# Two more pairs of steps with seven block products for the last matrix product, and block sums made from tiles that are already loaded

## The chip, the cores and the metric

The kernel runs on one core of a Trainium2 chip. The metric is the device time of one execution in microseconds (us). Three runs of the kernel before gave 736.80, 737.75 and 737.57 us, a median of 737.57 us.

The engines are named as in the profile. PE is TensorE (matrix products, results in PSUM), DVE is VectorE, ACT is ScalarE, POOL is GpSimd, and SP issues the DMAs. Each engine takes its instructions in a fixed order. One that waits holds up everything behind it on that engine.

## The reference, cut to what matters

```python
attn_out = _attn_ref(x, state)                 # attention both ways, (4, 8, 512+32, 64)
x = attn_out.transpose(0, 2, 1, 3).reshape(B * S, H * D)       # 2176 rows of 512
h = x @ w_in;  g = softplus(h);  x = g @ w_out                 # 512 -> 2048 -> 512
g = x @ w_gate                                                 # 512 -> 1536
silu = g * (1.0 / (1.0 + np.exp(-g)))
val = x @ w_val                                                # 512 -> 1536
return silu * val @ w_out2                                     # 1536 -> 512
```

The 2176 rows are 4 batches of 512 tokens and 128 state rows. The change lies in the last three products, which this text calls the gated stage.

## The kernel before

Every float32 operand is split into a high part and a low part in fp32r, and each product of tiles is three matmuls (high x high, low x high, high x low). The split costs two instructions: a copy on ACT for the high part (`h`) and a subtraction on DVE or POOL for the low part (`l`).

**The gated stage** begins at about 342 us and has 24 steps, numbered n = 0 to 23. Steps 0 to 11 do batches 0 and 1 (p = 0), steps 12 to 23 batches 2 and 3 (p = 1). One step does 128 of the 1536 columns of gate and of value for a pair of batches. It does so by a Strassen-Winograd scheme: seven block products P1 to P7, whose operands from the weights (`gw`) and from the activations (`T`: B11, B21, B22 and the sums T1 to T4) are prepared earlier. Each block product is six matmuls of 128x512, so a step has 42. They accumulate in three PSUM banks `px`, `pz`, `py`, in the order P1, P5, P2, P6, P7, P4, P3. DVE and ACT take the partial results out between them (tiles `cA`, `cB`, `cC`), and Silu and the product of gate and value follow in the next step.

**The last product** of two steps 2k, 2k+1 is done two steps later, in pieces put between the block products. It has two forms. The plain form, `out_mm`, has 24 matmuls in each of the two steps. The form with seven block products, `out_part`, has 18 in the even step (P1, P2, P5, six each) and 24 in the odd step (P6, P3, P7, P4). Its results for the two batches are kept in two pairs of banks: P1, P6, P7 and P4 follow each other in one pair, P2, P5 and P3 in the other, and after each part DVE adds the bank to `oacc`. A part that goes on in a bank can therefore not begin until DVE has read the part before it. This form also needs sums of the activations (`total`, on DVE, lines 994 to 1000 and 985) and sums of four blocks of w_out2 (`w2s`).

Before the change the seven-product form is used for steps 12 to 21, five pairs. The sums `w2s` are made by `OutSums` in steps 10, 12, 13, 14 and 16: two tiles `w2r` are loaded from DRAM, DVE adds high and low parts (`whole`, tiles `w2t`), POOL makes the sums (`w2u`), ACT and POOL split them, and the result is written to DRAM and loaded again by `load_w2s`.

**The sums T1 to T4 of the second pair of batches** are made from the result of the MLP before (`yacc`). `y_sums` does them in steps 9 and 10 (T3 and T2 on DVE, T1 and T4 on POOL); `y_high` and `y_low` split all seven operands in step 11.

**The 128 state rows** run beside steps 0 to 13: `state_1` is their gate and value (12 matmuls of 128x256 a step; Silu and the product are done once for two steps), `state_2` a transposition, `state_3` their last product.

The order on PE is that of the code. DVE, ACT, POOL and SP run in the order in which `run2(n, ...)`, `run_later(n, ...)` and `parts(n, ...)` put instructions between the block products: `conv0` stands after P2, `conv1` before P7, `state` and `conv2` after P7, `conv3` after P3. SBUF and PSUM addresses of the tiles are assigned when the program is built.

Of the kernel before, what the change touches and what calls it, by code (L numbers as in the profile page):

```python
# [37 lines left out]
def attention_moe_moe2_kernel(  # L38
# [38 lines left out]
    SLOTS = {"aT": 8, "mt": 8,  "wo": 6, "yacc": 8, "s": 2, "xT": 8, "T": 14, "made": 3, "w2": 4, "w2s": 4, "gw": 8}  # L77
# [36 lines left out]
    RAWS = {"raw": 2, "raw0": 6}  # L114
# [163 lines left out]
    def load_w2s(q):  # L278
        for k in range(2):
            w2s[q, k] = slot([P, 2, 512], F32R, "w2s", f"w2s{q}_{k}")  # L280
            nc.sync.dma_start(out=w2s[q, k].bitcast(F32), in_=w2s_d[q][:, k])
# [198 lines left out]
    y = {}  # L480
# [28 lines left out]
    def y_sums(p, i, k, eng):  # L509
        b11, b12, b21, b22 = (y_of(2 * p + j, 2 * h + i) for h in range(2) for j in range(2))  # L510
        if k == "T1":
            o = ysum[p, i, k] = b12
        else:
            o = ysum[p, i, k] = work.tile([P, 512], F32, tag="ysum", bufs=6, name=f"{k}_{p}_{i}")
        if k == "T3":
            eng.tensor_tensor(out=o, in0=b22, in1=b12, op=ALU.subtract)
        elif k == "T1":
            eng.tensor_tensor(out=o, in0=b12, in1=b11, op=ALU.subtract)
        elif k == "T2":
            eng.tensor_tensor(out=o, in0=ysum[p, i, "T3"], in1=b11, op=ALU.add)  # L520
        else:
            eng.tensor_tensor(out=o, in0=b21, in1=ysum[p, i, "T2"], op=ALU.subtract)
# [136 lines left out]
    def out_part(n, part):  # L659
# [8 lines left out]
        for i in range(2):  # L668
# [4 lines left out]
            w = w2s[q, k // 2] if kind == "s" else w2[n + int(kind[1])]  # L673
# [7 lines left out]
    def state_1(f):  # L681
        if f % 2 == 0:
            gs["t"] = bank("y", f"pt1{f}").rearrange("p (f s c) -> p f s c", f=2, s=2)
        ps = gs["t"][:, f % 2].rearrange("p s c -> p (s c)")
# [6 lines left out]
        if f % 2:  # L691
            pg, pv = (gs["t"][:, :, s, :] for s in range(2))
            t = work.tile([P, 2, 2 * P], F32, tag="sa", bufs=1, name=f"sa{f}")
            a, g = (t[:, k].rearrange("p (f c) -> p f c", f=2) for k in range(2))
            nc.scalar.activation(a, pg, AF.Silu)
            nc.vector.tensor_tensor(out=g, in0=pv, in1=a, op=ALU.mult)
            gs[f // 2] = t[:, 1]
# [12 lines left out]
    def state_3(q):  # L710
        ps = bank("y", f"pt3{q}")
# [18 lines left out]
    with tc.manual_schedule(engines={ENG.PE}):  # L730
# [244 lines left out]
        def value_times_gate(n, c):  # L975
# [5 lines left out]
            if n < NF or n >= NS2 - 2:  # L981
# [25 lines left out]
        with tc.manual_schedule(engines={ENG.DVE, ENG.SP, ENG.Activation, ENG.Pool}):  # L1007
            run2(-1, "load0")
            run2(-1, "load1")
            for n in range(NS2):  # L1010
# [10 lines left out]
                z = quad_bank(f"pz{n}")  # L1021
                quad_mm(z, n, "P5", True)
                run2(n, "P5")
                y = quad_bank(f"py{n}")
# [16 lines left out]
                else:  # L1041
# [8 lines left out]
                    parts(n, 0) if n >= NF + 2 else outs(n, 0)  # L1050
# [73 lines left out]
```

## Time and profile before

| | |
|---|---|
| median of three runs | 737.57 us |
| the profiled execution | 737.21 us, span 735.4 us |
| granted TensorE clock | 0.995, one core |
| PE busy | 710.3 us (97%) |
| DVE busy | 488.1 us (66%) |
| POOL busy | 441.7 us (60%) |
| ACT busy | 329.0 us (45%) |

The span runs from the first to the last instruction. The execution's own time is 1.8 us longer. A matmul's time in a row includes its way through the array, so a row of three that lists 0.84 us can be followed by the next row 0.68 us later: intervals between starts tell what each one costs. The same holds for DVE, where an instruction with 0.68 us is followed 0.60 us later by the next.

### The profile page before, as it was taken

How to read it: one execution, taken by the hardware profiler on the slowest of the kernel's cores; microseconds unless marked ns; L12 is line 12 of the kernel's file. 1: busy time of each engine (PE TensorE's matmuls, PEld its weight loads, DVE VectorE, ACT ScalarE, POOL GpSimd, SP SyncE). 2: the span in 40 equal slices, each digit the busy share in tenths (PEclk: the TensorE clock that was granted, in tenths of full speed). 3: DMA queues.
4: the chain of work that ended last, by engine and by line, in shares of the span. 5: the costliest groups of instructions: out<-in, count | busy, mean ns of one | idle time of the engine just before them, and what ended most of it. 6: DMA issues, size and time to landing. Idle time of an engine off the chain costs nothing.

```text
span 735.4 us, 10173 instructions
## 1 busy us (share of the span) xinstructions
PE 710.3 (97%) x3610; PEld 561.7 (76%) x3610; DVE 488.1 (66%) x665; ACT 329.0 (45%) x611; POOL 441.7 (60%) x397
## 2 busy tenths in 40 slices
PE   4699999999999999999999999999999999999997
PEld 1367767786777777788887888888888888888886
DVE  5984559888676878466575656665575665675564
ACT  3767445644544545434454434442443434333231
POOL 2467637887556775754396756766767567254352
PEclk9999999999999999999999999999999999999999
DMA  9930215655453535380379987979669997838503
GB/s 342 407 125 0 87 58 172 191 206 176 141 174 138 189 131 180 128 322 1 101 275 356 377 328 269 352 258 328 199 254 379 340 349 280 313 128 326 178 1 115
DMA packets 55395, 159.53 MB, mean 217 GB/s; under 512 B 6192, under 2 KB 18480, under 8 KB 55344
## 3 DMA queue, kind: packets, MB, share of 16 engines
q1 hardware_dynamic: 55344, 158.88, 60.9%
q8 instruction: 28, 0.46, 0.3%
q14 instruction: 23, 0.19, 0.1%
HBM read 117.70 MB, written 41.16 MB: 216 GB/s over the span
## 4 chain that ended last, share of the span: by engine, by line
PE 82%; POOL 3%; issue 2%; ACT 2%; DMA 2%; DVE 1%; SPq 0%; DVEq 0%; ACTq 0%; POOLq 0%
PE py L90 25%; PE px L90 16%; PE ph L90 10%; PE po L90 9%; PE pz L90 8%; PE poP L90 6%; PE pt L90 3%; PE ps L552 2%; PE pm L421 2%; PE ps L90 1%; DMA gv_d<-gv 1%; POOL l L93 1%; DMA raw_gv<-in_moe_w_gate_dram 1%; POOL gv L93 1%; POOL sums_gv L194 1%
## 5 line engine op out<-in xcount | busy, mean ns | idle before, releaser
L90 PE MATMUL py<-h,wo 128*128 128x512 f32 x512 | 158.8, 391 | 2.6 <-DVE yacc L500 1.3
L93 POOL TENSOR_TENSOR l<-C,h 128x512 fp32r<-128x512 f32 x64 | 94.1, 1476 | 78.7 <-PE py L90 51.6
L90 PEld LDWEIGHTS py<-h,wo 128*128 128x128 f32 x512 | 95.9, 188 | 23.9 <-POOL wo L93 2.0
L90 PE MATMUL ph<-aT,m 128*128 128x512 f32 x384 | 101.3, 399 | 1.0 <-DVE m L93 1.0
L90 PE MATMUL py<-l,wo 128*128 128x512 f32 x256 | 99.9, 390 | 0.0
L90 PEld LDWEIGHTS ph<-aT,m 128*128 128x128 f32 x384 | 70.8, 188 | 24.9 <-issue 6.9
L90 PE MATMUL po<-h,w 128*128 128x512 f32 x224 | 69.6, 392 | 0.0
L451 ACT ACTIVATE h<-ph 128x512 fp32r<-128x512 f32 x64 | 38.2, 597 | 68.3 <-PE ph L90 45.9
L90 PE MATMUL px<-T_0s,gw 128*128 128x512 f32 x216 | 60.8, 390 | 0.8 <-ACT cB L1047 0.8
L90 PE MATMUL px<-T_1s,gw 128*128 128x512 f32 x216 | 60.7, 389 | 0.0
L90 PEld LDWEIGHTS py<-l,wo 128*128 128x128 f32 x256 | 48.1, 188 | 10.5 <-POOL l L93 0.3
L90 PEld LDWEIGHTS po<-h,w 128*128 128x128 f32 x224 | 41.6, 188 | 8.4
L635 DVE TENSOR_TENSOR oacc<-po,oacc 128x512 f32<-128x512 f32 x48 | 32.4, 687 | 22.9 <-PE po L90 22.8
L635 DVE TENSOR_TENSOR oacc<-poP,oacc 128x512 f32<-128x512 f32 x62 | 40.7, 686 | 10.3 <-PE poP L90 10.3
L90 PEld LDWEIGHTS px<-T_0s,gw 128*128 128x128 f32 x216 | 40.3, 188 | 9.4 <-ACT cB L1047 1.2
L90 PEld LDWEIGHTS px<-T_1s,gw 128*128 128x128 f32 x216 | 40.6, 188 | 8.5
L93 POOL TENSOR_TENSOR l<-cA,h 128x512 fp32r<-128x512 f32 x14 | 21.4, 1528 | 38.2 <-ACT h L621 38.2
L90 PE MATMUL po<-l,w 128*128 128x512 f32 x112 | 43.6, 390 | 0.0
L93 POOL TENSOR_TENSOR split_gv<-sums_gv,split_gv 128x512 fp32r<-128x512 f32 x24 | 33.0, 1376 | 16.4 <-ACT split_gv L198 16.4
L500 DVE TENSOR_TENSOR yacc<-py,yacc 128x512 f32<-128x512 f32 x48 | 31.3, 685 | 16.7 <-PE py L90 16.7
L93 POOL TENSOR_TENSOR gv<-t_gv,gv 128x512 fp32r<-128x512 f32 x24 | 33.4, 1393 | 14.2 <-issue 11.7
L137 DVE TENSOR_SCALAR t_gv<-t_gv 128x512 int32<-128x512 int32 x24 | 22.1, 920 | 28.2 <-ACT t_gv L133 28.1
(192 smaller groups left out, 1538.5 us busy)
## 6 DMA issues: line engine op xcount, KB each, us to landing
gw<-gv_d SPq DMA_DIRECT2D x96, 512.0 KB, 6.9
gv_d<-gv SPq DMA_DIRECT2D x24, 512.0 KB, 3.9
gv_d<-split_gv SPq DMA_DIRECT2D x24, 512.0 KB, 3.2
w<-w_d SPq DMA_DIRECT2D x24, 512.0 KB, 8.4
raw_win<-in_moe_w_in_dram SPq DMA_DIRECT2D x16, 512.0 KB, 6.9
raw_wo<-in_moe_w_out_dram SPq DMA_DIRECT2D x16, 512.0 KB, 4.1
raw_gv<-in_moe_w_gate_dram SPq DMA_DIRECT2D x48, 128.0 KB, 3.8
raw_gv<-in_moe_w_val_dram SPq DMA_DIRECT2D x48, 128.0 KB, 3.6
```

What stands on the lines that cost most here:

```text
L90: nc.tensor.matmul(o, a[s], b[t], start=first and i == 0, stop=last and i == 2, **k)
L93: eng.tensor_tensor(out=o, in0=whole, in1=high.bitcast(F32), op=ALU.subtract)
L137: nc.vector.tensor_scalar(out=ti, in0=ti, scalar1=3, scalar2=0x7FFFFFF8, op0=ALU.logical_shift_left, op1=ALU.bitwise_and,)
L194: nc.gpsimd.tensor_tensor(out=o, in0=x, in1=y, op=op)
L421: nc.tensor.matmul(ps[k * NS:(k + 1) * NS, :], st[q, k, b, :], win[c, k].t[q, :], start=True, stop=True)
L451: nc.scalar.activation(self.h, self.ps, AF.Softplus)
L500: nc.vector.tensor_tensor(out=v, in0=yps[dt], in1=v, op=ALU.add)
L552: nc.tensor.matmul(ps, sw[:, kt, :], win[c, kt].t, start=kt == 0, stop=kt == KT - 1)
L635: nc.vector.tensor_tensor(out=v, in0=ps, in1=v, op=ALU.add)
```

## The change

The constant `FROM = 8` and `seven(n)` make `out_part` the form for steps 8 to 21, seven pairs instead of five. The pairs 8, 9 and 10, 11 belong to the first pair of batches; their parts run in steps 10 to 13.

`OutSums` no longer loads or stores anything. It reads the tiles `w2[n]`, `w2[n+1]` that are loaded for the last product anyway, and leaves its results in SBUF tiles `w2s`. It runs in the odd step n+1 of each pair: 9, 11, 13, 15, 17, 19, 21. Seven such jobs stand where five were, and the DMAs of `w2r`, `w2o` and `w2s` are gone.

T2 and T4 of the second pair of batches overwrite `yacc`. The sums and splits of that pair are spread over steps 9 to 12 by a table; T4 moves from POOL to DVE, and the tags that share SBUF and PSUM space are changed (`T` 16 slots, `raw2`, `quad_bank`). `state_1` works step by step in a bank of its own, with one Silu and one product of 128x128 in each.

```diff
-        def __init__(self, q):
-            self.q = q
-            self.raw = []
-            for f in range(2):
-                t = slot([P, 2, 512], F32R, "made", f"w2r{q}_{f}")
-                nc.sync.dma_start(out=t.bitcast(F32), in_=w2_d[2 * q + f])
-                self.raw.append(t)
+        def __init__(self, n):
+            self.n = n
 
         def whole(self):
             self.t = []
-            for f, r in enumerate(self.raw):
-                t = rawp.tile([P, 512], F32, tag="tmade", bufs=3, name=f"w2t{self.q}_{f}")
+            for f in range(2):
+                r = w2[self.n + f]
+                t = rawp.tile([P, 512], F32, tag="tmade", bufs=3, name=f"w2t{self.n}_{f}")
                 nc.vector.tensor_tensor(out=t, in0=r[:, 0].bitcast(F32), in1=r[:, 1].bitcast(F32), op=ALU.add)
                 self.t.append(t)
...
         def low(self):
-            w2s_d[self.q] = dram.tile([P, 2, 2, 512], F32, tag=f"w2s{self.q}", name=f"w2s{self.q}_d")
-            for k, o in enumerate(self.o):
+            for k in range(2):
+                o = w2s[self.n, k]
                 low(nc.gpsimd, o[:, 1, :], self.s[k], o[:, 0, :])
-                nc.sync.dma_start(out=w2s_d[self.q][:, k], in_=o.bitcast(F32))
...
@@ y_sums
+        elif p and k in ("T2", "T4"):
+            o = ysum[p, i, k] = b11 if k == "T2" else b21
...
@@ quad_bank
-    def quad_bank(name):
-        banks[0] += 1
-        return bank("h" if banks[0] % 4 else "m", name)
+    def quad_bank(name, state):
+        banks[0] += not state
+        return bank("h" if state or banks[0] % 4 else "m", name)
...
@@ state_1
+        if f % 2 == 0:
+            gs[f // 2] = work.tile([P, 2, 2 * P], F32, tag="sa", bufs=1, name=f"sa{f}")[:, 1]
+        g = gs[f // 2][:, f % 2 * P:(f % 2 + 1) * P]
+        nc.scalar.activation(g, ps[:, :P], AF.Silu)
+        nc.vector.tensor_tensor(out=g, in0=ps[:, P:], in1=g, op=ALU.mult)
...
-                for k, (t, eng) in enumerate((("T3", nc.vector), ("T1", nc.gpsimd), ("T2", nc.vector), ("T4", nc.gpsimd))):
-                    at2(n0 - 3 + i, f"conv{k}", y_sums, p, i, t, eng)
-            for part, (_, t) in PARTS.items():
+                for k, (t, eng) in enumerate((("T3", nc.vector), ("T1", nc.gpsimd))):
+                    at2(n0 - 3 + i, f"conv{2 * k + 1 - i}", y_sums, p, i, t, eng)
+            for t, early, high, then in (
+                ("B11", 1, "P5", "P2"), ("T1", 0, "P5", "P2"), ("B21", 0, "P2", "P6"), ("T2", 0, "P6", "P7"),
...
                 for i in range(2):
-                    at2(n0 - 1, part, y_high, p, i, t)
-                    at2(n0 - 1, part, y_low, p, i, t, nc.gpsimd if t in ("B21", "T3", "B22") else nc.vector)
+                    at2(n0 - 1 - early, high, y_high, p, i, t)
+                for i in range(2):
+                    at2(n0 - 1 - early, then, y_low, p, i, t, nc.gpsimd if t in ("B21", "T3", "B22") else nc.vector)
+            for i in range(2):
+                at2(n0 - 2, "P4", y_sums, p, i, "T2", nc.vector)
+                at2(n0 - 1, "P7", y_sums, p, i, "T4", nc.vector)
...
+        FROM = 8
+        def seven(n):
+            return FROM <= n < NS2 - 2
...
-        for q, n in enumerate((10, 12, 13, 14, 16)):
-            job = {}
-            at2(n - 1, "load1", lambda q=q, job=job: job.update(s=OutSums(q)))
-            for kind, name in (("conv0", "whole"), ("conv1", "sums"), ("conv2", "high"), ("conv2", "low")):
-                at2(n, kind, lambda name=name, job=job: getattr(job["s"], name)())
+        for n in range(0, NS2, 2):
+            if seven(n):
+                job = OutSums(n)
+                for kind, name in (("conv0", "whole"), ("conv1", "sums"), ("conv2", "high"), ("conv2", "low")):
+                    at2(n + 1, kind, getattr(job, name))
...
-            if n < NF or n >= NS2 - 2:
+            if not seven(n):
                 after(n + 1, 1, lambda: split_act((n, 1), c["C"]))
...
-                    parts(n, 0) if n >= NF + 2 else outs(n, 0)
+                    parts(n, 0) if seven(n - 2) else outs(n, 0)
```

Two places show how it moves instructions. The first is the end of step 11 on PE, where the last product of steps 8 and 9 stands. Before, it reads so (`po8_1_2` is the bank for batch 1, third quarter; `px11` takes P4 of the gate product, `pz11` P3, `px12` opens step 12):

```order
L90 MATMUL po8_1_2_5218<-h8_1_4868,w28_4633 128x512 x2
L90 MATMUL po8_1_2_5218<-l8_1_4869,w28_4633 128x512
L90 MATMUL po8_1_2_5218<-h9_1_5018,w29_4635 128x512 x2
L90 MATMUL po8_1_2_5218<-l9_1_5019,w29_4635 128x512
L90 MATMUL po8_1_3_5226<-h8_1_4868,w28_4633 128x512 x2
L90 MATMUL po8_1_3_5226<-l8_1_4869,w28_4633 128x512
L90 MATMUL po8_1_3_5226<-h9_1_5018,w29_4635 128x512 x2
L90 MATMUL po8_1_3_5226<-l9_1_5019,w29_4635 128x512
L90 MATMUL px11_5104<-T4_0_0s_3309,gw11_0_0_4934 128x512 x3
L90 MATMUL px11_5104<-T4_0_1s_3348,gw11_1_0_4936 128x512 x3
L90 MATMUL pz11_5120<-B22_0_0s_3156,gw11_0_1_4938 128x512 x3
L90 MATMUL pz11_5120<-B22_0_1s_3221,gw11_1_1_4940 128x512 x3
```

After, the same place has the parts P7 and P4 (`poP1_8` is the pair of banks that P1 opened; `h8_T3` and `h8_T4` are the split sums of activations):

```order
L90 MATMUL poP1_8_0_5014<-h8_T3_5097,w2s8_1_4919 128x512 x2
L90 MATMUL poP1_8_0_5014<-l8_T3_5098,w2s8_1_4919 128x512
L90 MATMUL poP1_8_1_5019<-h8_T3_5097,w2s8_1_4919 128x512 x2
L90 MATMUL poP1_8_1_5019<-l8_T3_5098,w2s8_1_4919 128x512
L90 MATMUL px11_5121<-T4_0_0s_3309,gw11_0_0_4958 128x512 x3
L90 MATMUL px11_5121<-T4_0_1s_3348,gw11_1_0_4960 128x512 x3
L90 MATMUL poP1_8_0_5014<-h8_T4_5129,w29_4647 128x512 x2
L90 MATMUL poP1_8_0_5014<-l8_T4_5130,w29_4647 128x512
L90 MATMUL poP1_8_1_5019<-h8_T4_5129,w29_4647 128x512 x2
L90 MATMUL poP1_8_1_5019<-l8_T4_5130,w29_4647 128x512
L90 MATMUL pz11_5135<-B22_0_0s_3156,gw11_0_1_4962 128x512 x3
L90 MATMUL pz11_5135<-B22_0_1s_3221,gw11_1_1_4964 128x512 x3
```

Eight rows with twelve matmuls of the plain form became P7 in front of `px11` and P4 behind it; P7 and P4 write the same two banks, with only `px11`'s six matmuls between them.

The second place is DVE in step 11. Before, between the adds of step 10's last results and the product for the state rows, it had these rows (`cB10<-pz10` is the last add of step 10, the rows `B11_1`, `T1_1`, `T2_1` are low parts for the second pair of batches, `sa11` the state rows):

```order
L1061 TENSOR_TENSOR cA10_4946<-px10_4949,cA10_4946 128x512
L1069 TENSOR_TENSOR cB10_4947<-pz10_4959,cB10_4947 128x512
L93 TENSOR_TENSOR B11_1_0s_5114<-yacc2_0_1137,B11_1_0s_5114 128x512
L93 TENSOR_TENSOR B11_1_1s_5117<-yacc2_0_1137,B11_1_1s_5117 128x512
L93 TENSOR_TENSOR T1_1_0s_5127<-yacc3_0_1356,T1_1_0s_5127 128x512
L93 TENSOR_TENSOR T1_1_1s_5130<-yacc3_0_1356,T1_1_1s_5130 128x512
L1044 TENSOR_TENSOR cA11_5101<-py11_5133,cA11_5101 128x512
L93 TENSOR_TENSOR T2_1_0s_5155<-T2_1_0_4896,T2_1_0s_5155 128x512
L93 TENSOR_TENSOR T2_1_1s_5158<-T2_1_1_5042,T2_1_1s_5158 128x512
L635 TENSOR_TENSOR oacc1_0_3851<-po8_1_0_5161,oacc1_0_3851 128x512
L635 TENSOR_TENSOR oacc1_0_3851<-po8_1_1_5169,oacc1_0_3851 128x512
L696 TENSOR_TENSOR sa11_5206<-pt110_5022,sa11_5206 128x256
```

After, what stands between the same add and the state rows is this (`w2t10` is `whole` for w_out2, `yacc2_1` the sum T4, `cB10<-cC10,cA10` a sum of activations):

```order
L1068 TENSOR_TENSOR cB10_4971<-pz10_4983,cB10_4971 128x512
L249 TENSOR_TENSOR w2t10_0_5153<-w210_4966 128x512
L249 TENSOR_TENSOR w2t10_1_5155<-w211_4968 128x512
L1043 TENSOR_TENSOR cA11_5118<-py11_5146,cA11_5118 128x512
L93 TENSOR_TENSOR T1_1_0s_5142<-yacc3_0_1356,T1_1_0s_5142 128x512
L93 TENSOR_TENSOR T1_1_1s_5144<-yacc3_0_1356,T1_1_1s_5144 128x512
L626 TENSOR_TENSOR oacc1_0_3857<-poP1_8_0_5014,oacc1_0_3857 128x512
L626 TENSOR_TENSOR oacc1_0_3857<-poP1_8_1_5019,oacc1_0_3857 128x512
L972 TENSOR_TENSOR cB10_4971<-cC10_4972,cA10_4970 128x512
L93 TENSOR_TENSOR T2_1_0s_5174<-yacc2_0_1137,T2_1_0s_5174 128x512
L93 TENSOR_TENSOR T2_1_1s_5176<-yacc2_0_1137,T2_1_1s_5176 128x512
L513 TENSOR_TENSOR yacc2_1_1140<-yacc2_1_1140,yacc2_0_1137 128x512 x2
```

Besides the low parts, the two adds of `w2t10`, a sum of activations and the two sums T4 now stand here; in front of `cB10<-pz10` three more sums of the kind SBUF with SBUF follow the adds of part P5 (`cA9<-cA9,cA8` and the two sums T2). Behind the last row stand the state rows (two), `cC11`, the two adds of P3 and then the add that reads P7's first bank.

## Rows read from the trace of the kernel before

**Rows 1.** The page: busy us, share of the span and instructions of each engine.

```profile
PE 710.3 (97%) x3610; PEld 561.7 (76%) x3610; DVE 488.1 (66%) x665; ACT 329.0 (45%) x611; POOL 441.7 (60%) x397
```

**Rows 2.** Waits of TensorE from 341 us on: total us, times, longest.

```profile
PE px L90 <- ACT cB L1047: 0.8, 1, 0.8
PE pz L90 <- DVE cC L1039: 0.5, 1, 0.5
```

**Rows 3.** Windows: steps 10 and 11, and the pair 14, 15.

```profile
core 0: us, PE busy (x) PEld busy (x) DVE busy (x) ACT busy (x) POOL busy (x), PEclk, DMA share, GB/s
511.42:528.04 16.62, 16.62 (x81) 14.05 (x80) 11.65 (x13) 5.53 (x11) 13.49 (x11) 1.00 0.63 238
528.04:545.82 17.78, 17.78 (x85) 14.95 (x84) 11.72 (x16) 9.36 (x19) 10.93 (x8) 1.00 0.67 206
570.74:599.30 28.56, 28.56 (x127) 23.66 (x127) 17.43 (x25) 11.73 (x21) 19.75 (x17) 1.00 0.98 332
```

**Rows 4.** Timeline of TensorE in step 10: start, duration, engine, line, operation.

```profile
511.42 0.84 PE L90 MATMUL px<-B_0s,gw 128*128 128x512 f32 x3
512.10 0.84 PE L90 MATMUL px<-B_1s,gw 128*128 128x512 f32 x3
...
516.86 0.62 PE L90 MATMUL po<-h,w 128*128 128x512 f32 x2
517.31 0.39 PE L90 MATMUL po<-l,w 128*128 128x512 f32 x1
517.54 0.62 PE L90 MATMUL po<-h,w 128*128 128x512 f32 x2
```

**Rows 5.** Timeline of VectorE, steps 10 to 12.

```profile
512.23 1.36 DVE L516 TENSOR_TENSOR T<-yacc,yacc 128x512 f32<-128x512 f32 x1
513.51 3.47 DVE L254 TENSOR_TENSOR w2t<-w2r 128x512 f32<-128x512 f32 x2
...
524.14 1.47 DVE L520 TENSOR_TENSOR T<-T,yacc 128x512 f32<-128x512 f32 x1
...
531.33 1.37 DVE L93 TENSOR_TENSOR B_0s<-yacc,B_0s 128x512 fp32r<-128x512 f32 x1 [2.40 <-ACT B_0s L532]
532.62 0.68 DVE L93 TENSOR_TENSOR B_1s<-yacc,B_1s 128x512 fp32r<-128x512 f32 x1
533.23 0.68 DVE L93 TENSOR_TENSOR T_0s<-yacc,T_0s 128x512 fp32r<-128x512 f32 x1
533.83 1.78 DVE L93 TENSOR_TENSOR T_1s<-yacc,T_1s 128x512 fp32r<-128x512 f32 x1
...
547.87 1.77 DVE L93 TENSOR_TENSOR T_1s<-T,T_1s 128x512 fp32r<-128x512 f32 x1
...
550.17 2.88 DVE L254 TENSOR_TENSOR w2t<-w2r 128x512 f32<-128x512 f32 x2
```

**Rows 6.** Timeline of GpSimd beside them.

```profile
511.75 1.29 POOL L93 TENSOR_TENSOR l<-cA,h 128x512 fp32r<-128x512 f32 x1 [5.91 <-ACT h L621]
513.00 1.74 POOL L522 TENSOR_TENSOR T<-yacc,T 128x512 f32<-128x512 f32 x1
...
518.09 0.74 POOL L265 TENSOR_TENSOR w2u<-w2t,w2t 128x256 f32<-128x256 f32 x1
```

**Rows 7.** Groups of VectorE from 341 us: busy us, mean ns, idle before.

```profile
L635 DVE TENSOR_TENSOR oacc<-poP,oacc 128x512 f32<-128x512 f32 x62 | 40.7, 686 | 10.3 <-PE poP L90 10.3
...
L254 DVE TENSOR_TENSOR w2t<-w2r 128x512 f32<-128x512 f32 x10 | 11.5, 1186 | 0.0
...
L973 DVE TENSOR_TENSOR cA<-cA,cA 128x512 f32<-128x512 f32 x5 | 6.1, 1219 | 0.0
...
L973 DVE TENSOR_TENSOR cB<-cC,cA 128x512 f32<-128x512 f32 x5 | 3.4, 683 | 0.0
...
L696 DVE TENSOR_TENSOR sa<-pt,sa 128x256 f32<-128x256 f32 x6 | 2.5, 420 | 5.4 <-ACT sa L695 5.0 <-POOL l L93 0.4
```

**Rows 8.** DMA issues from 341 us: count, KB each, us to landing.

```profile
w2s<-w2s_d SPq DMA_DIRECT2D x10, 512.0 KB, 9.0
```

More of the change, by code (lines that the diff above doesn't have):

```diff
@@ L74, in attention_moe_moe2_kernel @@
     psum = ctx.enter_context(tc.tile_pool(name="psum", bufs=1, space=bass.MemoryType.PSUM))
[L77 removed]
+    SLOTS = {"aT": 8, "mt": 8,  "wo": 6, "yacc": 8, "s": 2, "xT": 8, "T": 16, "made": 3, "w2": 4, "w2s": 4, "gw": 8}
     def slot(shape, dt, tag, name):
@@ L203, in __init__ @@
         def __init__(self, f):
-            super().__init__([w_out2[f * P:(f + 1) * P, :]], "made", f"w2{f}")
+            super().__init__([w_out2[f * P:(f + 1) * P, :]], "made", f"w2{f}", "raw2")
             self.f = f
@@ L258, in sums @@
             (a11, a21), (a12, a22) = ((t[:, :256], t[:, 256:]) for t in self.t)
-            self.s = [rawp.tile([P, 512], F32, tag="sums", bufs=2, name=f"w2u{self.q}_{k}") for k in range(2)]
+            self.s = [rawp.tile([P, 512], F32, tag="sums", bufs=2, name=f"w2u{self.n}_{k}") for k in range(2)]
             s = [self.s[k // 2][:, k % 2 * 256:(k % 2 + 1) * 256] for k in range(4)]
@@ L267, in high @@
         def high(self):
-            self.o = [slot([P, 2, 512], F32R, "made", f"w2o{self.q}_{k}") for k in range(2)]
-            for k, o in enumerate(self.o):
+            for k in range(2):
+                o = w2s[self.n, k] = slot([P, 2, 512], F32R, "w2s", f"w2s{self.n}_{k}")
                 nc.scalar.activation(o[:, 0, :], self.s[k], AF.Copy)
         def low(self):
-            w2s_d[self.q] = dram.tile([P, 2, 2, 512], F32, tag=f"w2s{self.q}", name=f"w2s{self.q}_d")
-            for k, o in enumerate(self.o):
+            for k in range(2):
+                o = w2s[self.n, k]
                 low(nc.gpsimd, o[:, 1, :], self.s[k], o[:, 0, :])
-                nc.sync.dma_start(out=w2s_d[self.q][:, k], in_=o.bitcast(F32))
[L278 to L281, printed above, removed]
     win = {}
@@ L672, in out_part @@
             c = slice(k % 2 * 256 + i * P, k % 2 * 256 + (i + 1) * P)
-            w = w2s[q, k // 2] if kind == "s" else w2[n + int(kind[1])]
+            w = w2s[n, k // 2] if kind == "s" else w2[n + int(kind[1])]
             mm3(ps, [w[:, l, c] for l in range(2)], act[n, t], opens, True, skip_group_check=True)
@@ L681, in state_1 @@
     def state_1(f):
-        if f % 2 == 0:
-            gs["t"] = bank("y", f"pt1{f}").rearrange("p (f s c) -> p f s c", f=2, s=2)
-        ps = gs["t"][:, f % 2].rearrange("p s c -> p (s c)")
+        ps = bank("m", f"pt1{f}")[:, :2 * P]
         for dt in range(KT):
@@ L690, in state_1 @@
             )
[L691 to L697, printed above, removed]
+        if f % 2 == 0:
[3 more added lines that the diff above has]
+        nc.vector.tensor_tensor(out=g, in0=ps[:, P:], in1=g, op=ALU.mult)
     def state_2(q):
-        ps = bank("y", f"pts{q}")
+        ps = bank("m", f"pts{q}")
         for i in range(2):
@@ L710, in state_3 @@
     def state_3(q):
-        ps = bank("y", f"pt3{q}")
+        ps = bank("m", f"pt3{q}")
         for f in range(2):
@@ L1058, in attention_moe_moe2_kernel @@
                 run2(n, "conv2")
-                parts(n, 1) if n >= NF + 2 else outs(n, 2)
+                parts(n, 1) if seven(n - 2) else outs(n, 2)
                 quad_mm(x, n, "P4", False)
                 nc.vector.tensor_tensor(out=c["A"], in0=x, in1=c["A"], op=ALU.mult)
-                split_act((n, 0) if n < NF or n >= NS2 - 2 else (n - n % 2, ("B11", "B21")[n % 2]), c["A"])
-                if n >= NF + 2:
+                split_act((n - n % 2, ("B11", "B21")[n % 2]) if seven(n) else (n, 0), c["A"])
+                if seven(n - 2):
                     parts(n, 2)
```

15 lines of the change are left out of this document (7 added, 8 removed).

## The prediction

> **What bounds the kernel now.** I read the busy shares first. PE works for 710.3 of 735.4 us, DVE for 488.1, POOL for 441.7 [rows 1]. A share over the whole span hides stages, so I read next the waits of PE in the gated stage: two, of 0.8 and 0.5 us, in 394 us [rows 2]. The windows of the steps that the change touches show PE busy for the whole of each, 16.62 of 16.62 and 17.78 of 17.78 us, at a granted clock of 1.00, that is 2.4 GHz [rows 3]. So a matmul saved here is time saved, and a wait put on PE here is time lost. No other engine can be hidden behind anything: only its slack counts. DVE has 16.62 - 11.65 = 5.0 us of it in step 10 and 17.78 - 11.72 = 6.1 in step 11; POOL 3.1 and 6.9 [rows 3].
>
> **What a matmul costs.** A half product of three matmuls begins 0.68 us after the one before (511.42, 512.10), and so do the three of the last product (516.86 with 517.31, then 517.54) [rows 4]: 0.2267 us each. It checks: a pair of steps with seven-product parts has 2 x 42 + 42 = 126 such matmuls, 28.56 us [rows 3].
>
> **Part 1, fewer matmuls.** Two pairs of steps go from 48 to 42 matmuls, six each, both of them in the even step (24 to 18). That is 12 x 0.2267 = 2.72 us off, 1.36 in step 10 and 1.36 in step 12. Both lie in stretches where PE never waits, so the gain is certain as far as nothing new is late. Step 10 becomes 16.62 - 1.36 = 15.26 us long; step 11 keeps its 66 matmuls and 17.78 us.
>
> **Part 2, the queue of DVE in step 11.** The new form ties PE to DVE. The part P4 writes the bank that P7 used, so its first matmul waits until DVE has added P7's first half to `oacc`. Before, no out product waited like that in steps 10 to 13: each had a bank of its own. I follow DVE's queue, on the clock of the trace before (PE's times until 511.42 taken as they were).
>
> When DVE gets free: part P5 is the last but one piece of step 10 and ends at 511.42 + 15.26 - 1.36 = 525.32. The last result is there 0.16 us after PE goes on (the row of 517.31 with its 0.39 us ends at 517.70, the next begins at 517.54 [rows 4]); the second add takes 0.60 us until the next instruction can follow: 526.1.
>
> When PE wants P4's part: step 11 begins at 526.68, P4's part stands 1.36 + 1.36 before its end: 526.68 + 17.78 - 2.72 = 541.74.
>
> Between the two DVE has 22 instructions to do, as the order of the change shows. Twelve read two SBUF tiles: one sum for the activations and the two sums T2 at the end of step 10, the two `w2t` adds, two low parts of T1, one more activation sum, two low parts of T2, two sums T4. Nine read PSUM or are adds to `oacc`; they cost 0.60 us each when they follow each other (532.62 to 533.23 is such an interval [rows 5]; the group of 62 adds has 686 ns on the mean, as much as one alone [rows 7]). One is the state rows' product of half the former size, between 0.2 and 0.42 [rows 7], 0.3 taken. Fixed part: 9 x 0.60 + 0.3 = 5.7. With c for each of the twelve the queue takes 5.7 + 12c, and there are 541.74 - 526.1 = 15.6 us. So **c = 0.83 us is where PE begins to wait**, and every 0.1 us above it costs 1.2 us.
>
> What c is: with POOL idle such an instruction takes 0.68, an interval of 0.60 (532.62, 533.23). With POOL at work it takes 1.36 to 1.78: the two `w2t` adds of 513.51 took 3.47 together, beside POOL instructions that took 1.74 where they take 1.29 alone [rows 5, 6]. The eleven in rows 5 sum to 15.46 us, 1.41 each, or 1.33 from start to start. The group of ten `w2t` adds has a mean of 1.186, the five sums `cA<-cA,cA` 1.219, the five `cB<-cC,cA`, which POOL's pauses happen to cover, 0.683 [rows 7]. Ends: 0.60 and 1.70. POOL's own queue beside these twelve has 13 instructions (low parts of activations, the product of gate and value, two B21 low parts, four `w2u`, two `w2s`), some 9 x 1.29 + 4 x 0.74 = 14.6 us alone [rows 6] in 15.6 us, so it hardly pauses. I take 1.25, between the groups' 1.2 and the 1.33 of rows 5: 5.7 + 15.0 - 15.6 = **5.1 us of waiting on PE**. The range by c is 0 to 10.5.
>
> The Trainium skill, page "SBUF — State Buffer", section "Who interferes with whom", says that an instruction of DVE with two SBUF inputs contends with one of GpSimd that reads SBUF, under an exclusive lock, and one with a single SBUF input does not. The trace agrees on both kinds (1.70 against 0.686). By that rule each of the twelve could stand behind a whole POOL instruction, 1.29 + 0.60 = 1.89 as an estimate, and PE would wait for 12.8 us; the rows of before stop at 1.78, and rival (c) has their price.
>
> **Part 3, what follows in step 12.** DVE leaves the wait late, and behind it come the two low parts of T4, two sums for the activations and the adds of P1's and P2's parts. POOL in that time does T3, B22 and the product of gate and value. P5's part of step 12 waits for DVE's add as well, and PE may lose up to two contended instructions' excess, 2 x 0.9 = 1.8; at best 0. I take 0.5.
>
> **Part 4, sums of w_out2 in place.** Seven jobs instead of five: two DVE adds, four POOL instructions of 0.74, two copies and two low parts each. Two of them stand in steps 9 and 11; that of step 11 is counted above. In steps 13 to 21 they move within a pair of steps in which DVE works 17.43 of 28.56 us [rows 3]. The two adds come before `cA<-py`, whose reader is Silu on ACT and not PE. I cost it 0; if the place is bad, four pairs lose up to 0.5 each, 2.0. The 30 DMAs of `w2r`, `w2o` and `w2s` go [rows 8]. PE waited for none, so 0 gained.
>
> **Part 5, the rest.** State rows: one more bank, six more Silu and six more products of half the size, about 6 x 0.3 = 1.8 us on DVE over 12 steps, with 5 us of slack or more in such a step [rows 3]; 0, at worst 0.5. Banks by other tags: the two waits of rows 2 could vanish or one more like them appear, -1.3 to +0.8; 0 taken.
>
> **Sum.** -2.72 + 5.1 + 0.5 = +2.9 us. On the profiled execution's 737.21 us this is 740.1; that execution lies 0.36 under the median of the runs, so about **740.5 us**.
>
> **Rivals.**
> (a) VectorE keeps up. c stays at or below 0.83 because DVE and POOL settle into each other's pauses, as the `cB<-cC,cA` sums do at 0.683 [rows 7]; P4's part never waits. For it: nine of 22 instructions do not care about POOL, and they spread the twelve. Against it: rows 5, where 9 of 11 were slow. Time: 737.57 - 2.72 = 734.85. This is the case on the other side, and it decides at c = 0.83.
> (b) Wait and saving cancel. c between 0.89 and 1.13: a wait of 0.7 to 3.7 in step 11 and 0.5 in step 12, less 2.72, within 1.5 us of before: 737.6. For it: the two cheap rows in rows 5, and instructions that wait for ACT while POOL finishes.
> (c) Full alternation. POOL never pauses and each of the twelve meets one of its instructions: c = 1.70 as in the pair at 513.51 [rows 5], 5.7 + 20.4 - 15.6 = 10.5 of wait, with 0.5 behind it +8.3: 745.9. Against it: four of POOL's instructions are 128x256, of 0.74, and a wait on PE also starves POOL of work.
> The Trainium skill's rule above speaks for it, with a chance no higher than the rows allow.
> (d) P5's part in step 10 waits for `w2s`, which POOL has not split in time. POOL gets 4 x 0.74 + 2 x 1.29 = 5.5 us more to do in step 9 [rows 6], against 3.1 us of slack in step 10 [rows 3]: a wait of 2.4 at most, and with no other -2.72 + 2.4, 737.3. It lies inside (b).
>
> **Chances.** Forecast (c from 1.13 to 1.5, +1.5 to +5.9): 0.44. (a) 0.26. (b) with (d) 0.19. (c) 0.11. What a measurement of this kernel can tell from no change is about 0.2%, 1.5 us. Faster 0.26, same 0.19, slower 0.55. The likeliest case alone reaches from 739.1 to 743.5. The range has to take in (a), with 0.3 below it for a better bank order, and most of the forecast's upper side: 734.5 to 744.0, which leaves out (c) and a few in the hundred below.
>
> **What would show it.** Right: PE's waits from 341 us list one on `poP` from DVE `oacc`, 3 to 7 us, near 542 us, and the `w2t`, T2, T4 and activation sums of that stretch last 1.2 us or more; windows of steps 14 to 23 still have PE busy throughout. Part 1: step 10 takes 15.3 us. Wrong by (a): no wait in step 11 and a span of 732.7. Wrong in Part 4: waits in odd steps from 13 on. Wrong altogether: waits in steps 9 or 10 for `w2s`, or at the opening of a bank that the state rows use.

## The result, and the profile after

The changed kernel takes 743.15 us (four runs, 742.59 to 743.89) against 737.58 us before (four runs): a ratio of 1.0077, 95% interval 1.0064 to 1.0090. That is slower by 5.6 us. The forecast said slower with a chance of 0.55, at 740.5 us in a range of 734.5 to 744.0.

The page's first lines answer to [rows 1]. They show span and instructions, and then busy time, share of the span and instructions of each engine:

```profile
span 740.8 us, 10130 instructions
...
PE 713.1 (96%) x3598; PEld 561.5 (76%) x3598; DVE 508.6 (69%) x697; ACT 337.1 (46%) x627; POOL 461.4 (62%) x413
```

There are 12 matmuls fewer, 3598 for 3610, and yet PE is busy 2.8 us longer. A count that falls while its busy time rises says that some matmuls ran slower. The waits of PE from 341 us on come next (engine, line, what it waited for, total us, times, longest):

```profile
PE poP L90 <- DVE oacc L626: 5.4, 2, 5.2
PE px L90 <- ACT cB L1046: 0.9, 1, 0.9
PE pz L90 <- DVE cC L1038: 0.5, 1, 0.5
```

The last two are those of [rows 2]. The first is new: 5.24 us in front of part P4 in step 11, and 0.17 us in front of the second half of part P5 in step 12. The windows answer to [rows 3]; they are step 10, step 11, the stretch of step 11 after the wait, step 12, and a stretch of the later steps (from within step 13 to within step 15):

```profile
core 0: us, PE busy (x) PEld busy (x) DVE busy (x) ACT busy (x) POOL busy (x), PEclk, DMA share, GB/s
510.99:526.25 15.26, 15.26 (x75) 12.91 (x74) 11.33 (x18) 6.88 (x14) 9.02 (x7) 1.00 0.66 215
526.25:552.40 26.15, 20.80 (x85) 16.55 (x84) 23.40 (x26) 11.04 (x21) 21.03 (x16) 0.87 0.29 102
547.12:552.40 5.28, 5.28 (x12) 4.12 (x13) 2.53 (x4) 1.68 (x3) 3.40 (x3) 0.50 0.04 5
552.40:566.83 14.43, 14.26 (x64) 11.35 (x63) 9.13 (x15) 6.34 (x12) 7.01 (x7) 1.00 0.52 179
576.00:605.30 29.30, 29.30 (x131) 24.27 (x130) 19.89 (x29) 10.13 (x19) 17.93 (x16) 1.00 0.72 243
```

Step 10 has lost what it should, 16.62 to 15.26 us. Step 11 has grown from 17.78 to 26.15, and the third window tells why the wait alone does not make that up. After the wait PE ran at a granted clock of 0.50, which is 1.2 GHz, and 12 matmuls took 5.28 us where at full clock they take 2.72. The timeline of PE shows the place (start, duration, operation, wait before it):

```profile
540.36 0.84 PE L90 MATMUL px<-T_0s,gw 128*128 128x512 f32 x3
541.03 0.84 PE L90 MATMUL px<-T_1s,gw 128*128 128x512 f32 x3
547.12 1.22 PE L90 MATMUL poP<-h_T,w 128*128 128x512 f32 x2 [5.24 <-DVE oacc L626]
...
551.12 1.44 PE L90 MATMUL pz<-B_1s,gw 128*128 128x512 f32 x3
552.40 0.87 PE L90 MATMUL px<-B_0s,gw 128*128 128x512 f32 x3
```

Three matmuls that begin at 551.12 are followed at 552.40, 1.28 us later; before the wait they took 0.68. DVE's timeline from the last add of P5's part to P4's wait is the queue that the prediction counted:

```profile
524.46 1.33 DVE L626 TENSOR_TENSOR oacc<-poP,oacc 128x512 f32<-128x512 f32 x2
525.70 1.42 DVE L972 TENSOR_TENSOR cA<-cA,cA 128x512 f32<-128x512 f32 x1
527.05 2.38 DVE L511 TENSOR_TENSOR yacc<-T,yacc 128x512 f32<-128x512 f32 x2
529.35 0.68 DVE L1068 TENSOR_TENSOR cB<-pz,cB 128x512 f32<-128x512 f32 x1
529.95 2.89 DVE L249 TENSOR_TENSOR w2t<-w 128x512 f32<-128x512 f32 x2
...
534.46 1.79 DVE L93 TENSOR_TENSOR T_1s<-yacc,T_1s 128x512 fp32r<-128x512 f32 x1
536.17 1.27 DVE L626 TENSOR_TENSOR oacc<-poP,oacc 128x512 f32<-128x512 f32 x2
537.37 0.83 DVE L972 TENSOR_TENSOR cB<-cC,cA 128x512 f32<-128x512 f32 x1
538.13 1.22 DVE L93 TENSOR_TENSOR T_0s<-yacc,T_0s 128x512 fp32r<-128x512 f32 x1
539.28 1.23 DVE L93 TENSOR_TENSOR T_1s<-yacc,T_1s 128x512 fp32r<-128x512 f32 x1
540.43 3.45 DVE L513 TENSOR_TENSOR yacc<-yacc,yacc 128x512 f32<-128x512 f32 x2
543.80 0.28 DVE L684 TENSOR_TENSOR sa<-pt,sa 128x128 f32<-128x128 f32 x1
...
545.19 2.47 DVE L626 TENSOR_TENSOR oacc<-poP,oacc 128x512 f32<-128x512 f32 x4
```

GpSimd's own timeline beside the end of that queue:

```profile
536.92 0.74 POOL L260 TENSOR_TENSOR w2u<-w2u,w2t 128x256 f32<-128x256 f32 x1
537.62 1.19 POOL L260 TENSOR_TENSOR w2u<-w2t 128x256 f32<-128x256 f32 x1
538.77 1.19 POOL L260 TENSOR_TENSOR w2u<-w2t,w2u 128x256 f32<-128x256 f32 x1
539.91 1.75 POOL L93 TENSOR_TENSOR l_T<-cB,h_T 128x512 fp32r<-128x512 f32 x1
541.62 3.38 POOL L93 TENSOR_TENSOR w2s<-w2u,w2s 128x512 fp32r<-128x512 f32 x2
```

DVE has no idle time in 21 us. By starts, the twelve instructions with two SBUF inputs take 1.35 + 2.30 + 2.81 + 2.80 + 0.76 + 2.30 + 3.37 = 15.69 us, 1.31 each, and the third of the four adds at 545.19 is the one that frees P4's part at 547.

**Where the 5.8 us of PE's last matmuls (730.83 to 736.61) came from.** Differences of step lengths, before and after: up to the start of step 9 -0.43 (493.64 to 493.21, not the change's doing, since the runs here differ by that much and more), step 9 none, step 10 -1.36, step 11 +8.37, step 12 -0.81 (15.24 to 14.43), steps 13 to 23 within 0.02. Step 11's +8.37 is 5.41 of waiting (541.03 + 0.68 to 547.12), 5.28 - 2.72 = 2.56 of low clock, and 0.40 where the copy cB on ACT held up P7 of the gate product.

### The profile page after: what moved, and what is told of

Its sections match the earlier page's. It is cut to its first block, busy times and chain, and to the rows that moved or that the text cites. A ratio compares the mean times of both kernels' runs of the same rounds, so it can differ in the third digit from the quotient of the medians.

```text
span 740.8 us, 10130 instructions
## 1 busy us (share of the span) xinstructions
PE 713.1 (96%) x3598; PEld 561.5 (76%) x3598; DVE 508.6 (69%) x697; ACT 337.1 (46%) x627; POOL 461.4 (62%) x413
## 4 chain that ended last, share of the span: by engine, by line
PE 77%; DVE 10%; POOL 5%; issue 3%; ACT 3%; DMA 1%; SPq 0%; DVEq 0%; ACTq 0%; POOLq 0%
PE py L90 24%; PE px L90 14%; PE ph L90 9%; PE poP L90 8%; PE pz L90 8%; PE po L90 6%; PE pt L90 2%; PE ps L543 2%; PE pm L410 2%; POOL sums_gv L194 1%; DVE oacc L626 1%; POOL l L93 1%; PE ps L90 1%; POOL gv L93 1%; POOL split_gv L93 1%
## 5 line engine op out<-in xcount | busy, mean ns | idle before, releaser
L93 POOL TENSOR_TENSOR l<-C,h 128x512 fp32r<-128x512 f32 x64 | 91.1, 1428 | 87.0 <-ACT C L443 74.3
L626 DVE TENSOR_TENSOR oacc<-poP,oacc 128x512 f32<-128x512 f32 x90 | 59.0, 686 | 13.5 <-PE poP L90 13.4
L90 PE MATMUL po<-h,w 128*128 128x512 f32 x160 | 49.7, 392 | 0.0
L93 POOL TENSOR_TENSOR l_T<-cA,h_T 128x512 fp32r<-128x512 f32 x14 | 19.3, 1382 | 42.1 <-ACT h_T L612 31.0
L137 DVE TENSOR_SCALAR t_gv<-t_gv 128x512 int32<-128x512 int32 x24 | 24.5, 1022 | 30.4 <-ACT t_gv L133 30.3
L977 POOL TENSOR_TENSOR cC<-cC,cB 128x512 f32<-128x512 f32 x24 | 31.7, 1319 | 16.8 <-ACT cB L976 16.8
L443 ACT ACTIVATE C<-ph 128x512 f32<-128x512 f32 x64 | 37.9, 593 | 0.0
L1043 DVE TENSOR_TENSOR cA<-py,cA 128x512 f32<-128x512 f32 x22 | 15.1, 686 | 29.9 <-PE py L90 29.8
```

What stands on the lines that cost most here:

```text
L90: nc.tensor.matmul(o, a[s], b[t], start=first and i == 0, stop=last and i == 2, **k)
L93: eng.tensor_tensor(out=o, in0=whole, in1=high.bitcast(F32), op=ALU.subtract)
L137: nc.vector.tensor_scalar(out=ti, in0=ti, scalar1=3, scalar2=0x7FFFFFF8, op0=ALU.logical_shift_left, op1=ALU.bitwise_and,)
L443: nc.scalar.activation(self.g, self.ps, AF.Softplus)
L626: nc.vector.tensor_tensor(out=v, in0=ps, in1=v, op=ALU.add)
L977: nc.gpsimd.tensor_tensor(out=c["C"], in0=c["C"], in1=c["B"], op=ALU.mult)
```

## The experiments

Theory A is that of the prediction with the clock added: DVE's queue, made long by GpSimd beside it, makes P4's part in step 11 late, and the wait lowers TensorE's clock. Theory B: many small costs of the rest of the change. Rival C: DVE has too many instructions there, whatever GpSimd does. Rival D came later: work that is put off is missed elsewhere. Rival E: the low clock has another cause than the wait. The runs of before that went with them have medians of 737.28 to 737.67 us.

**1. The rest of the change alone.**

```diff
-        FROM = 8
+        FROM = 12
```

> FROM = 12: all of the change stays (sums of w_out2 in place, T2 and T4 in yacc, banks, state rows step by step), only the parts of the pairs 8 and 10 go back to the plain form. Theory A (what costs is DVE's queue in front of part P4 in step 11, and TensorE's clock after that wait): no wait on poP, clock 1.00 throughout, 3308 matmuls as before, 737.0 to 738.2 us. Theory B (the in-place sums, the banks or the state rows cost, in many small places): stays over 740 us with waits in several odd steps.

737.79 us (ratio 1.0010, 1.0001 to 1.0019). PE has the two old waits and nothing else, 3610 matmuls as before (the expectation's 3308 is a slip), and every step from 4 to 22 is as long as before to 0.02 us. So the in-place sums, the banks, the state rows and the spread of T1 to T4 cost about 0.5 us together (0.1 to 1.4 by the interval), and hardly any of it in PE's steps. Theory B is out for the 5.6 us.

**2. Two sums moved off the queue.**

```diff
+                for i in range(2 if t == "T4" else 0):
+                    at2(n0 - 1, "P4", y_sums, p, i, "T4", nc.vector)
                 for i in range(2):
                     at2(n0 - 1 - early, high, y_high, p, i, t)
...
-                at2(n0 - 1, "P7", y_sums, p, i, "T4", nc.vector)
```

> The two sums T4 move on DVE from in front of part P4's wait in step 11 to behind part P4's adds; nothing else. They took 3.37 us there. Theory A: the wait of 5.24 us falls by 2.6 to 3.4, to 1.8 to 2.6 us; if the lower clock after it comes with any wait, 2.6 us stay with it and the time is about 740.2; if it comes only with a longer wait, 737.6. Theory B: nothing changes, 743.

738.88 us (ratio 1.0023, 1.0014 to 1.0033). The wait fell from 5.24 to 1.9 us, by the 3.37 us that the two sums had taken. The low clock came with this shorter wait too, in a smaller stretch:

```profile
545.50:549.13 3.63, 3.63 (x10) 2.86 (x9) 3.04 (x5) 1.26 (x2) 2.56 (x2) 0.54 0.30 118
```

Part of P4's part and P3 took 1.6 us more than at full clock. Of the 4.3 us gained, about 3.4 are the wait and 1.0 the clock. Neither of the two times that theory A gave came, since the lower clock cost neither 2.6 us nor nothing.

**3. The same queue on DVE, without GpSimd beside its end.**

```diff
-                for kind, name in (("conv0", "whole"), ("conv1", "sums"), ("conv2", "high"), ("conv2", "low")):
-                    at2(n + 1, kind, getattr(job, name))
+                late = (("conv0", "whole", 1), ("P4", "sums", 1), ("P1", "high", 2), ("P1", "low", 2))
+                usual = (("conv0", "whole", 1), ("conv1", "sums", 1), ("conv2", "high", 1), ("conv2", "low", 1))
+                for kind, name, d in late if n == 10 else usual:
+                    at2(n + d, kind, getattr(job, name))
```

> DVE's order is that of the changed kernel; only the job of GpSimd for the pair 10 (four sums w2u, and the splitting of w2s) moves from the middle of step 11 to behind part P4. Theory A with contention: the five instructions of DVE that stood beside it (a sum of activations, T2 low parts, T4 sums, 6.4 us) fall to 0.6 to 0.8 each, the wait to 2.2 to 3.2 us. Rival C (DVE simply has too many instructions, whatever GpSimd does): wait stays 5.2 us, time 743.

The wait fell to 2.9 us, with DVE's order unchanged. The five instructions that had stood beside the moved job, in the order of the timeline above from 537.37 on:

```profile
537.32 0.68 DVE L974 TENSOR_TENSOR cB<-cC,cA 128x512 f32<-128x512 f32 x1
537.91 0.68 DVE L93 TENSOR_TENSOR T_0s<-yacc,T_0s 128x512 fp32r<-128x512 f32 x1
538.52 0.68 DVE L93 TENSOR_TENSOR T_1s<-yacc,T_1s 128x512 fp32r<-128x512 f32 x1
539.12 2.38 DVE L513 TENSOR_TENSOR yacc<-yacc,yacc 128x512 f32<-128x512 f32 x2
541.42 0.28 DVE L684 TENSOR_TENSOR sa<-pt,sa 128x128 f32<-128x128 f32 x1
```

The five need 4.10 us (537.32 to 541.42, where the state rows' product begins) instead of 6.43 (537.37 to 543.80): 2.33 us, which is what the wait lost. Three of them fell to 0.60 from start to start; the two sums T4 took 1.15 each, with one low part still on GpSimd at 538.74. Rival C is out as a full account: the count matters, and so does what GpSimd does beside it. The time fell only to 741.88 us (ratio 1.0070, 1.0048 to 1.0092), since GpSimd's work that was put off stretched two sums of activations in step 12 to 1.67 us each on DVE, and P5's part there waited 1.6 us for the state rows' split that follows them.

**4. A first plan for step 11.** The edit is that of run 2, and in the table of the second pair of batches

```diff
-                ("B11", 1, "P5", "P2"), ("T1", 0, "P5", "P2"), ("B21", 0, "P2", "P6"), ("T2", 0, "P6", "P7"),
+                ("B11", 1, "P5", "P2"), ("T1", 0, "P6", "P7"), ("B21", 0, "P6", "P7"), ("T2", 0, "P6", "P4"),
```

> In step 11, T2's low parts and T4's sums move behind part P4's adds, and the copies of T1 and B21 on ACT move behind the copy cB (which was 0.26 us late for TensorE). DVE has 8 in place of 12 instructions with two SBUF inputs in front of P4's part: 5.7 + 8 x 1.31 = 16.2 us against 15.6. Theory A: a wait of 0 to 0.8 us, clock 1.00, 735.0 to 736.0 us. Theory B: over 740.

740.41 us (ratio 1.0043, 1.0028 to 1.0058), a miss. The wait on P4's part was 1.3 us with no low clock after it. But DVE had now waited 1.9 us itself, for the state rows' Silu, since ACT did ten copies in a row ahead of it:

```profile
541.43 0.29 DVE L684 TENSOR_TENSOR sa<-pt,sa 128x128 f32<-128x128 f32 x1 [1.92 <-ACT sa L683]
```

and T4's copies, which now wait for the late sums, stood on ACT in front of cA of step 12, for which PE waited 1.8 us; a stretch of low clock followed (0.50 in 555.24:558.50).

**5. A second plan.** Against the changed kernel: T4's sums as in run 2, and

```diff
-                ("B11", 1, "P5", "P2"), ("T1", 0, "P5", "P2"), ("B21", 0, "P2", "P6"), ("T2", 0, "P6", "P7"),
-                ("T3", 0, "P7", "P4"), ("T4", 0, "P4", "P3"), ("B22", -1, "P1", "P5"),
+                ("B11", 1, "P5", "P2"), ("T1", 0, "P5", "P2"), ("B21", 0, "P6", "P7"), ("T2", 0, "P7", "P4"),
+                ("T3", 0, "P4", "P4"), ("T4", -1, "P5", "P2"), ("B22", -1, "P1", "P5"),
```

> All of the change, with step 11's sums and splits for the second pair of batches placed anew: T2's low parts and T4's sums stand behind part P4's adds on DVE, and the copies on ACT are ordered so that neither cB of step 11, nor the state rows' Silu, nor cA of step 12 stands behind one that waits (B21 behind cB, T2 behind C's copy, T3 behind P4, T4 in step 12). Theory A: in front of P4's part DVE has 8 instructions with two SBUF inputs, and no idle time of 1.9 us for the Silu as in the fourth run; the wait there was 1.3 us, so it should go to 0 or nearly; no low clock; the saving of 2.72 us comes out: 734.3 to 735.5 us. Rival D (the work that was put off is missed in step 12, as in the fourth run): a wait of 1 to 2 us in step 12 with 1.6 us of low clock, 737 to 739.

740.95 us (ratio 1.0056, 1.0043 to 1.0068). Both numbers were too low, theory A's 734.3 to 735.5 and rival D's 737 to 739. Rival D was right in kind, but the low clock that it counted did not come. The waits:

```profile
PE px L90 <- ACT cB L1047: 2.5, 2, 1.8
PE poP L90 <- DVE tsh L93: 2.1, 1, 2.1
PE poP L90 <- DVE oacc L626: 1.3, 2, 1.0
```

The add cB of step 11, behind T2's and T4's work on DVE, came so late that ACT waited 3.25 us for it, and the copies of T4 stood in front of ACT's copy cB of step 12 this time, for which PE waited 1.8 us. DVE itself waited 1.66 us for T4's copies, spent 3.2 us on T4's low parts, and came to the sums of activations only after them and the adds of P1's part; the copies of these and the split `tsh` followed late, and P5's part waits for that split because its first half takes over its bank.

**6. One pair only.**

```diff
-        FROM = 8
+        FROM = 10
```

> FROM = 10: only the pair 10, 11 is added (six matmuls fewer, in step 12); step 11 has plain out products with banks of their own, which no add on DVE holds up, though the w_out2 sums of that pair still stand in its queue. Theory A: no wait in step 11, -1.36 us against the run with FROM = 12 (737.8), perhaps +0.3 in step 12: 736.2 to 736.8. Theory B: near 740.

737.79 us (ratio 1.0008, 0.9999 to 1.0016): step 11 had no wait on an out product, as expected, but the saving did not come. P5's part of step 12 waited for `tsh` here too:

```profile
558.68 0.73 PE L90 MATMUL poP<-h_T,w2s 128*128 128x512 f32 x2 [1.15 <-DVE tsh L93]
```

By starts, step 12 took 15.83 us, 1.95 more than the 13.88 that its count of matmuls asks for: 1.3 at this wait, the rest mostly behind it, where the second half of P5's part waited for DVE's add. Step 11 was 0.68 longer than before, most of it where the gate product's P3 waited for DVE's cC. Together that is more than the 1.36 us saved, and the interval of the time includes no change. So even a single pair meets a wait in step 12, and the queue on DVE is late for PE without an out product to wait for it.

**7. The wait by itself.** In the kernel of run 1, far from the state rows:

```diff
         def whole(self):
+            for _ in range(5 if self.n == 16 else 0):
+                for f in range(2):
+                    r = w2[self.n + f]
+                    t = rawp.tile([P, 512], F32, tag="tmade", bufs=3, name=f"w2t{self.n}_{f}")
+                    nc.vector.tensor_tensor(out=t, in0=r[:, 0].bitcast(F32), in1=r[:, 1].bitcast(F32), op=ALU.add)
             self.t = []
```

> FROM = 12 (which had no wait and 737.8 us), and in step 17, far from the state rows and the second pair's sums, DVE does the two adds w2t five more times: ten more instructions with two SBUF inputs in front of part P4. This measures a wait on that part by itself. Theory A: PE waits for oacc on poP in step 17 for some 3 to 8 us, and the clock is at half speed for some 3 to 5 us after it, so the time rises by 1.6 to 2.6 us more than the wait. Rival E (the low clock in step 11 has another cause, such as the state rows' products before it): the time rises by the wait alone.

The wait fell on P7's part, which waits for the adds of P6's part in the same way, and the clock fell after it:

```profile
628.14 0.39 PE L90 MATMUL poP<-l_B,w2s 128*128 128x512 f32 x1
631.37 1.22 PE L90 MATMUL poP<-h_T,w2s 128*128 128x512 f32 x2 [2.84 <-DVE oacc L631]
632.39 0.63 PE L90 MATMUL poP<-l_T,w2s 128*128 128x512 f32 x1
632.81 1.05 PE L90 MATMUL poP<-h_T,w2s 128*128 128x512 f32 x2
```

Step 17 took 19.46 us (618.84:638.30) against 14.96 in run 1: 3.0 of waiting (628.37 to 631.37) and 1.5 of low clock, a little under the 1.6 to 2.6 expected. Rival E is out: a wait made in another step, by another cause, is followed by the same. The time is 741.18 us, 3.4 above run 1. The spans of the two profiled executions differ by 3.0 us and not by 4.5, since in this one step 12 began 0.48 us sooner and the span ended 1.0 us sooner after the last matmul.

**8. A third plan, by what 4 to 6 showed.** Against the changed kernel:

```diff
-                for k, (t, eng) in enumerate((("T3", nc.vector), ("T1", nc.gpsimd))):
-                    at2(n0 - 3 + i, f"conv{2 * k + 1 - i}", y_sums, p, i, t, eng)
+                at2(n0 - 3 + i, f"conv{1 - i}", y_sums, p, i, "T3", nc.vector)
+                at2(n0 - 3 + i, f"conv{3 - 2 * i}", y_sums, p, i, "T1", nc.gpsimd)
...
-                ("B11", 1, "P5", "P2"), ("T1", 0, "P5", "P2"), ("B21", 0, "P2", "P6"), ("T2", 0, "P6", "P7"),
-                ("T3", 0, "P7", "P4"), ("T4", 0, "P4", "P3"), ("B22", -1, "P1", "P5"),
+                ("B11", 1, "P5", "P2"), ("T1", 0, "P5", "P2"), ("B21", 0, "P6", "P7"), ("T2", 0, "P6", "P7"),
+                ("T3", 0, "P4", "P3"), ("T4", -1, "P2", "P6"), ("B22", -1, "P1", "P5"),
...
+                for i in range(2 if t == "T4" else 0):
+                    at2(n0 - 1, "P3", y_sums, p, i, "T4", nc.vector)
...
-                at2(n0 - 2, "P4", y_sums, p, i, "T2", nc.vector)
-                at2(n0 - 1, "P7", y_sums, p, i, "T4", nc.vector)
+                at2(n0 - 2, "P7", y_sums, p, i, "T2", nc.vector)
...
-            at2(2 * q + 2, "state", state_2, q)
+            at2(2 * q + 2, "conv1" if q == NQ - 1 else "state", state_2, q)
```

> FROM = 8 again, step 11 planned by what the runs before showed. T1's second sum and both sums T2 go into step 10's pauses of GpSimd and VectorE, T4's sums behind the last add of step 11 (so that this add and what hangs on it are not late), its copies behind the next step's second product, T3's copies behind part P4, and the state rows' transposition of step 12 in front of P7, so that part P5 there does not wait for its split. In front of P4's part 8 of 12 instructions with two SBUF inputs are left, in step 12 nothing waits behind late work. Theory A: no wait over 0.6 us on poP, clock 1.00, and the saving of 2.72 us appears: 734.5 to 736.0 us. Rival D (DVE's work of these steps fits nowhere without a wait): one wait of 1 us or more moves to another place, 737 or more.

735.37 us against 737.67 before: a ratio of 0.9970, 0.9960 to 0.9981. It beats both kernels. Its waits from 341 us, and steps 10 to 12:

```profile
PE px L90 <- ACT cB L1047: 0.6, 1, 0.6
PE pz L90 <- DVE cC L1039: 0.5, 1, 0.5
PE poP L90 <- DVE oacc L626: 0.4, 1, 0.4
```

```profile
510.57:525.84 15.27, 15.27 (x76) 12.92 (x75) 12.62 (x20) 6.87 (x14) 8.80 (x7) 1.00 0.62 206
525.84:544.25 18.41, 18.06 (x85) 14.87 (x84) 17.95 (x22) 9.86 (x19) 17.65 (x14) 1.00 0.38 132
544.25:558.13 13.88, 13.88 (x64) 11.44 (x62) 13.14 (x18) 7.62 (x15) 11.44 (x9) 1.00 0.60 210
```

Steps 10 and 12 are 1.36 us shorter than before, as the count of matmuls says, step 11 is 0.63 longer, and the clock is 1.00 in all three: 2.1 us less in PE's steps. The two sums T2 took 1.29 us together in step 10, most of it in a pause of GpSimd, instead of 2.38 in the queue.

## Why the prediction was right, and what it left out

**Part 1** was exact: -1.36 us in step 10. In step 12 it was there too, below what the waits added.

**Part 2** named the wait that came: place (P4's part, near 542), releaser (the add of P7's first bank) and size, 5.1 predicted and 5.24 in the waits, 5.41 by starts. c was taken as 1.25 and measured 1.31; the end of the queue's lead-in was predicted for 526.1 and came at 525.70 on a clock that ran 0.43 ahead. That the wait came out so near is in part luck, as two errors offset each other: twelve times 0.06 more makes the queue 0.7 us longer, and PE came to P4's part 0.40 us late itself, held up by cB. The eleven instructions of [rows 5] were a choice, too: three more of the kind in those steps, at 537.43, 538.04 and 546.58 of the trace before, bring the mean from start to start down from 1.33 to 1.23, close to the 1.25 taken. That c was the right number to argue about is shown by run 3, where GpSimd's work alone was moved. The twelve ranged from 0.76 to 1.71 from start to start. The Trainium skill's rule in "SBUF — State Buffer", section "Who interferes with whom", agrees in its kind: the 90 adds of `oacc` with one SBUF input have a mean of 686 ns as before, while the others lengthen; the longest, 1.79, comes near the estimate of 1.89 for a whole blocked instruction. But the estimate that all twelve would pay that was 12.8 us of wait; the measured 5.2 decides, and rival (c) with it.

**The term that was missing** is the clock. The sum had waits alone, and each was priced at its length. The wait of 5.24 us also cost 2.56 us afterwards, shown in the window at 0.50, and shown as a consequence of waiting by run 7. With it the sum is -2.72 + 5.41 + 0.40 + 2.56 + 0.55 = +6.2, less the 0.43 of the start: 5.8, as measured at PE's last matmuls. That is why the result lies 2.7 us above the forecast though the main wait was foreseen to 0.3 us. The likeliest case reached to 743.5 because c might have been 1.5, and c was 1.31: that 743.15 lies inside it is luck, since another cost than the one allowed for filled the room.

**Part 3** was set at 0.5 for step 12; it lost 0.55, and 0.48 of it, by starts, at P5's part, whose second half waited for DVE's add as foreseen (563.60 to 565.44 for six matmuls; 0.17 is what the list calls waiting). The 0.40 of cB in step 11 was not in the sum. Before, PE wanted the bank that ACT's copy cB empties 8.16 us into the step (536.20), and cB had ended at 6.34 us although six other copies stood in front of it. After, with six matmuls fewer in front, PE wants the bank at 6.81 us, and cB ended at 7.02: ACT had waited 1.13 us for the add cB of step 10, which stands in DVE's long queue, and then did four copies first. Run 4, with the four behind cB, had no such hold-up.

**Parts 4 and 5** were costed at 0 and came to about 0.5 (run 1).

**The rivals.** (a), VectorE keeps up, was wrong for this order; run 8 comes to its result, 0.4 us of wait apart, with the same sums made and eight instead of twelve of them in front of P4's part. (d), P5's part waiting for `w2s`, did not happen in any run; what P5's part waits for, when it does, is DVE: its first half for the state rows' split, its second for an add of P2's part. In the built program the part does not go on in P2's pair of banks for the pair 10: its first bank is that of the state rows' transposition, its second the first of P2's. I had not followed the wait for the split, and it undid runs 3, 5 and 6.

**Left open.** What decides whether a short wait lowers the clock (below). And the 0.5 us of run 1: its interval begins at 1.0001, so it may be next to nothing, and no run took the edits of Parts 4 and 5 apart. Part of it lies outside the span: what an execution takes beyond its span is 1.79 us before, 2.03 in run 1, 2.25 in the changed kernel and 2.39 in run 8 (medians), and no trace shows why. In run 8 the median span fell by 2.9 us, the time by 2.3.

## What to carry to other kernels

When a new order ties the bound engine to a second one, write down that engine's whole queue between the two events, with the price of each instruction beside its neighbour; two more instructions there cost 3.4 us on PE, and behind the event the same two cost PE nothing (run 2, where step 12 stayed at 14.4 us). Price a wait of TensorE above its length: here 5.24 us of waiting cost 2.56 us more, so look at the granted clock behind every wait. And after moving work out of a queue, follow every engine's order up to the next step, ACT's copies too, because the second wait is often behind the one that was removed.

## What the runs showed of the hardware that was not expected

TensorE's granted clock fell to 0.50 (1.2 GHz) after waits of 5.24 us (cost 2.56 us), 2.84 us (run 7, 1.5 us), 2.91 us (run 3, 1.65 us), 1.9 us (run 2, 1.6 us) and 1.8 us (run 4, 1.6 us), each time having been at 1.00 for hundreds of us before. It stayed at 1.00 after waits of 1.0 to 1.3 us (runs 4 to 6) and of 1.6 us (the second of run 3), but also in run 5 after 1.75 and 2.07 us within 9 us of each other. So a wait near 2 us may cost nearly twice its length, or only its length, and these runs do not tell which.
